# First three chunks projected from unpermuted weights by 32-column tiles, with the permutations behind them

## The chip, the cores and the metric

One core of one Trainium2 chip runs one program. The metric is the device time of that program in microseconds (us), and the figure of record is the median of several runs. TensorE (PE) multiplies matrices, its weight loads are shown as PEld; VectorE (DVE), ScalarE (ACT) and GpSimd (POOL) do the rest, and SyncE (SP) issues the transfers (DMAs).

## The reference

Four layers work on one sequence of 2048 tokens of width 576, in bfloat16: attention, gated linear unit (GLU), attention, GLU, each on a normalised input and added to it. The weights of the two attentions are the same, as are those of the two GLUs.

```python
def _A_ref(x, wqkv, wo):                 # 32 heads of 18, window of 8 at distance 2
    qkv = (x @ wqkv).reshape(B, S, 3, H, Dh)
    idx = pos[:, None] - (jnp.arange(8) * 2)[None, :]
    ...
    logits = jnp.einsum("bhsd,bhswd->bhsw", q, kg) * scale   # masked where idx < 0
    attn = softmax(logits)
    return einsum("bhsw,bhswd->bhsd", attn, vg).reshape(B, S, D) @ wo

def _B_ref(x, w_gate, w_up, w_down):     # F = 4608
    return ((x @ w_gate) * (x @ w_up)) @ w_down

x = x + _A_ref(_layernorm(x), wqkv, wo)
x = x + _B_ref(_layernorm(x), w_gate, w_up, w_down)
x = x + _A_ref(_layernorm(x), wqkv, wo)
x = x + _B_ref(_layernorm(x), w_gate, w_up, w_down)
```

## The kernel before

The sequence is cut into chunks of 128 tokens (the first four) or 256. For each chunk an attention and a GLU are made, and the chunks of the two layer pairs follow one another in one list, `seq`. All weights stay in SBUF: `wqkv` for the attention, `wg`, `wu` and `wgu_t` for the GLU (loaded in six slices of 768 columns, 0 to 5); the rows of w_down pass through seven buffers `wd`. Width 576 is four blocks of 128 rows and a tail of 64, so each contraction has four full matmuls (k = 0 to 3) and a half one.

The attention works with q, k and v in an order of columns in which the 18 elements of a head lie apart: column d * 32 + h in place of h * 18 + d. The kernel gets this order by permuting the weights once. `load_w` (L323) loads the raw `A_wqkv` into a scratch tile `scr` in two parts, "a" (q and k) and "b" (v), and `perm` in `setup_b` (L355) copies it, 512 columns of q, k or v at a time and the last 64 or 128 apart, with a read of every 18th element, into `wqkv`. DVE copies q and half of k, ACT the rest of k and all of v. `project` (L527) then multiplies: 14 column blocks of 128 per chunk, 56 full matmuls and 14 of 64 rows. For chunk 0 (`fast`) the q and k part runs k by k as the permuted blocks come, then the v part.

What follows for a chunk: eviction of q, k, v from PSUM (L609, L611, L638, L645); four products q*k for two window places each on DVE (L676), summed over d by PE with the selector `Esel` (L691, in tiles of 32 columns); softmax on DVE and ACT (L710 to L722); the weights spread over the heads' rows by PE with `Bsel` (L732) and copied back; eight products with v (L762), which for chunk 0 PE sums (L766, L767) and for others DVE; the output projection (L816), the residual (L786), statistics (L414, L418), normalisation (L439), transposes on PE (L452, L454) and their eviction (L457). Then the GLU: gate and up (L866, tails L877), `g_sb` (L901) and the product `h` (L902), down (L918, L919).

The order on every engine is not that of the source. Each step is an `op` with an engine, a cost in ns, what it reads and writes, a priority and a rank (the chunk's number; 0.5 for a permutation, 60 for GLU). `Plan.run` repeatedly takes the step that can start first by these costs, and holds a step of higher rank back if one of rank 0 or below would come within a guard time (`GUARD`). Where PE would stand idle, `fill` adds dummy matmuls (L1067). The result is written out in that order; at run time engines wait for one another by semaphores. All transfers of this stage go through SP's one queue, in order.

Chunks 0 to 4 have their input transposed on PE. Chunk 1's projection stands on PE just ahead of the first GLU matmul, those of chunks 2 and 3 follow behind the first six units of the GLU of chunk 0.

## Time and profile before

| what | value |
|---|---|
| three runs | 1060.21, 1063.39, 1062.1 us; median 1062.1 |
| profiled execution | 1063.46 us, span from first to last instruction 1061.7 us |
| granted PE clock, mean | 0.996 |
| PE, DVE, ACT busy | 98%, 74%, 39% of the span |
| DMA | 133.67 MB, mean 126 GB/s |

The profile is of one execution. Busy times are sums over instructions; matmuls overlap, and the end of one is modelled, so a stream of matmuls is read by its starts. A row of the timeline is start, duration, engine, line, operation, output and inputs, sizes, count, and in brackets the idle time ahead of it and what ended that. Lines are those of the kernel before; the changed kernel has other numbers (L527 becomes L610 for raw and L613 for permuted weights, L355 L417, L676 L762, L691 L777, L732 L818, L762 L850, L786 L874, L866 L954, L902 L990, L918 L1006).

### The profile page before, as it was taken

To read this page: it belongs to the slowest core of one execution; us is meant where nothing else is said; L and a number is where in the kernel's file an instruction comes from. 1 tells how busy PE (TensorE), PEld (TensorE's weight loads), DVE (VectorE), ACT (ScalarE), POOL (GpSimd) and SP (SyncE) were. 2 spreads that over 40 slices of the span, in tenths; PEclk is the share of its full clock that TensorE was granted. 3 is DMA by queue.
4 is the path that set the end of the run, shared out by engine and by line. 5 is a ranking of instruction groups with operands and counts; after the bars stand their busy time and mean duration, and the time that the engine had idled before them with its cause. 6 is when DMAs were issued, how large, how long until landed. Compare 5 with 4: busy or idle time off the path is not lost.

```text
span 1061.7 us, 39938 instructions
## 1 busy us (share of the span) xinstructions
PE 1044.4 (98%) x17864; PEld 839.5 (79%) x17864; DVE 781.6 (74%) x1421; ACT 411.8 (39%) x1090; POOL 8.9 (1%) x33
## 2 busy tenths in 40 slices
PE   7999999999999999999999999999999999999998
PEld 4888878798888878878878887777877778877775
DVE  7688979786969896989798874666788748833332
ACT  6752254342334534423444324324334252233231
POOL 3000000000000000000000000000000000000000
PEclk9999999999999999999999999999999999999999
DMA  9956563623253444345444443243362333443332
GB/s 263 323 184 197 179 178 102 170 69 121 81 147 86 128 103 109 82 126 138 117 93 106 110 143 94 83 147 87 75 173 82 94 94 115 126 127 102 114 102 68
DMA packets 146827, 133.67 MB, mean 126 GB/s; under 512 B 42272, under 2 KB 146016, under 8 KB 146656
## 3 DMA queue, kind: packets, MB, share of 16 engines
q1 hardware_dynamic: 146656, 131.13, 44.1%
q8 instruction: 139, 2.28, 0.9%
q14 instruction: 32, 0.26, 0.1%
HBM read 118.51 MB, written 4.06 MB: 115 GB/s over the span
## 4 chain that ended last, share of the span: by engine, by line
PE 77%; DVE 14%; DMA 5%; ACT 1%; SPq 1%; issue 1%; DVEq 0%; ACTq 0%
PE pu L890 15%; PE pg L890 13%; PE pu L958 5%; PE acct L890 4%; PE pa L958 4%; PE pa L890 4%; PE pg L527 4%; PE pu L527 3%; PE pg L958 3%; PE acct L958 3%; PE pu L866 3%; PE pg L866 3%; PE pg L918 3%; DVE scr L762 2%; DVE oT L776 2%; DVE h L902 2%
## 5 line engine op out<-in xcount | busy, mean ns | idle before, releaser
L890 PE MATMUL pg<-xnT_B,wg 64*128 64x256 bf16 x3072 | 394.8, 270 | 3.2 <-DVE xf L786 3.2
L890 PE MATMUL pu<-xnT_B,wu 64*128 64x256 bf16 x3072 | 394.3, 270 | 1.6 <-DVE xf L938 1.2
L890 PEld LDWEIGHTS <-wg 64*128 64x128 bf16 x4032 | 367.3, 94 | 28.6 <-issue 3.4
L890 PEld LDWEIGHTS <-wu 64*128 64x128 bf16 x4032 | 366.3, 94 | 24.6 <-issue 3.6
L902 DVE TENSOR_TENSOR h<-pu,g_sb 128x512 bf16<-128x512 f32 x228 | 153.7, 686 | 59.4 <-ACT g_sb L901 56.0
L958 PEld LDWEIGHTS <-h 64*128 64x128 bf16 (+1 forms) x1992 | 120.7, 94 | 96.9 <-DVE h L902 1.6
L901 ACT CAST g_sb<-pg 128x512 bf16<-128x512 f32 x228 | 132.2, 586 | 115.8 <-PE pg L890 80.6
L471 ACT COPY tok<-pu 1x1 f32<-1x1 f32 x270 | 39.7, 147 | 308.8 <-PE pu L890 214.5
L959 PE MATMUL pg<-wd,h 64*128 64x64 bf16 (+1 forms) x828 | 157.4, 190 | 1.4 <-DVE xf L786 1.4
L959 PE MATMUL pu<-wd,h 64*128 64x64 bf16 (+1 forms) x828 | 157.4, 190 | 0.3 <-DVE xf L786 0.2
L958 PE MATMUL pg<-wd,h 64*128 64x512 bf16 x600 | 154.9, 377 | 0.3 <-DVE h L902 0.3
L958 PE MATMUL pu<-wd,h 64*128 64x512 bf16 x600 | 154.9, 377 | 0.0
L890 PE MATMUL acct<-xnT_B,wg 64*128 64x256 bf16 x960 | 130.7, 269 | 0.0
L890 PE MATMUL pa<-xnT_B,wu 64*128 64x256 bf16 x960 | 130.7, 270 | 0.0
L959 PEld LDWEIGHTS <-h 64*128 64x128 bf16 (+1 forms) x1992 | 119.2, 95 | 2.1 <-issue 1.7
L527 PEld LDWEIGHTS <-wqkv 64*128 64x128 bf16 (+1 forms) x2044 | 103.9, 94 | 15.5 <-issue 3.8
L676 DVE TENSOR_TENSOR scr<-qT,kv 128x2560 bf16<-128x2560 bf16 (+1 forms) x68 | 89.9, 1326 | 29.9 <-ACT kv L611 29.7
L958 PE MATMUL acct<-wd,h 64*128 64x512 bf16 (+1 forms) x396 | 103.6, 382 | 0.4 <-DVE h L902 0.4
L958 PE MATMUL pa<-wd,h 64*128 64x512 bf16 (+1 forms) x396 | 104.0, 382 | 0.0
L890 PE MATMUL pu<-xnT_B,wgu_t 64*128 64x256 bf16 x384 | 103.5, 270 | 0.0
L890 PE MATMUL pg<-xnT_B,wgu_t 64*128 64x256 bf16 x384 | 103.5, 269 | 0.0
L527 PE MATMUL pg<-xnT_A,wqkv 64*128 64x256 bf16 (+2 forms) x853 | 96.3, 261 | 0.1
(155 smaller groups left out, 1645.9 us busy)
## 6 DMA issues: line engine op xcount, KB each, us to landing
wd<-in_B_w_down_dram SPq DMA_DIRECT2D x324, 288.0 KB, 4.5
scr<-a_dram SPq DMA_DIRECT2D x52, 128.0 KB, 2.8
wg<-in_B_w_gate_dram SPq DMA_DIRECT2D x6, 768.0 KB, 9.4
wu<-in_B_w_up_dram SPq DMA_DIRECT2D x6, 768.0 KB, 10.9
out_dram<-xf SPq DMA_DIRECT2D x16, 144.0 KB, 3.2
xb<-in_A_x_dram SPq DMA_DIRECT2D x6, 288.0 KB, 2.9
a_dram<-scr SPq DMA_DIRECT2D x13, 128.0 KB, 2.8
scr<-in_A_wqkv_dram SPq DMA_DIRECT2D x4, 288.0 KB, 4.3
```

Of the source, the lines that this page charges most:

```text
L471: box["at"] = nc.scalar.copy(tok[0:1, :], src())
L527: return nc.tensor.matmul(bank(p_, u)[0:m, e * n:(e + 1) * n], lhsT=wqkv[r_, k, w0:w0 + m], rhs=xnT_A[r_, k, c0:c0 + n], start=start, stop ...
L676: nc.vector.tensor_tensor(late["prod"][p_ % 2][:, :, :, 0:n], q2, k2, op=ALU.mult)
L762: nc.vector.tensor_tensor(js(dst), js(vT[:, :, o0:o0 + n]), abw, op=ALU.mult)
L776: op("DVE", 70 + 2.63 * n, lambda i_=i_: nc.vector.tensor_tensor(oT[:, :, 0:n], oT[:, :, 0:n], late["prod"][i_ % 2][:, 0, :, 0:n], op=ALU. ...
L866: nc.tensor.matmul(pt[:, e * n:(e + 1) * n], lhsT=w_[:, k, ft * P:(ft + 1) * P], rhs=xT[:, k, 0:n], start=(first and k == 0 and e == 0), s ...
L890: return nc.tensor.matmul(ps[:, e * n:(e + 1) * n], lhsT=w_, rhs=xT[rows, k, 0:n], start=(first and e == 0 and k == 0), stop=(not first an ...
L901: op("ACT", 490, lambda: nc.scalar.copy(g_sb[gs][:, 0:ul], pg[use["slot"]][:, 0:ul]), r=[f"wg_{j}_{u}"], w=[f"g{gs}"], prio=0, due=True)
L902: op("DVE", 605, lambda: nc.vector.tensor_tensor(hb[hs][:, 0:ul], pu[use["slot"]][:, 0:ul], g_sb[gs][:, 0:ul], op=ALU.mult), r=[f"wu_{j}_{ ...
L918: nc.tensor.matmul((pg, pu)[i][use["slot"]][:], lhsT=lhs, rhs=wt[:, e % 2, 0:512], start=first, stop=fin)
L958: return [lambda: nc.tensor.matmul((pg, pu)[i][use["slot"]][:], lhsT=lhs, rhs=wt[rows, e % 2, 0:512], start=first, stop=fin, skip_group_ch ...
L959: lambda: nc.tensor.matmul((pg, pu)[i][tl["slot"]][:, 0:TL], lhsT=lhs, rhs=wt[rows, e % 2, 512:D], start=first, stop=fin, skip_group_check ...
```

## The change

1. The raw weights are no longer in `scr` but in the place of the GLU weights' slices 4 and 5 (`raw`). Those slices' loads come later, after every use of the raw weights; `setup_glu` is split for this.
2. Chunks 0, 1 and 2 (`NRAW = 3`) project straight from the raw weights: each block of 128 columns is made by four matmuls of 32 columns into four 32-row parts of the bank, each with weights read at every 18th column (`raw32`).
3. The permutations get rank 1 and priority 6 and go, step by step, to DVE or ACT, whichever is free first (`alts`). Only chunk 3 and later read `wqkv`.
4. The planner first plans the operations of rank below 1 alone (`ahead`) and keeps the start of each as `res`; in the real pass an operation of a later rank may not be placed where it would run over such a place by more than `TOL`. Guards get shorter. Attentions of chunks 1 and 2 are put into the list ahead of GLU 0.
5. Small steps of chunk 0: statistics in single operations, normalisation and eviction of the GLU's input in two halves on ACT and DVE, four product buffers instead of two in the sum over v, x of chunk 1 loaded ahead of the weights, part "b" issued after the second instead of the third piece of "a".

```diff
-HOLD = 2
+HOLD = 1
-GUARD = {"DVE": 300, "ACT": 300, "PE": 600, "POOL": 0, "SP": 0}
+GUARD = {"DVE": 50, "ACT": 50, "PE": 100, "POOL": 0, "SP": 0}
+TOL = {"DVE": 100, "ACT": 100, "PE": 100, "POOL": 1e9, "SP": 1e9}
...
+    def ahead(self, slots, last):
+        every, emit = self.ops, self.fill
+        ops = [o for o in every if o.idx < last and o.rank < 1]
...
+        self.run(slots)
...
+        for o in ops:
+            if o.rank == 0 and o.cost and o.eng != "SP":
+                o.res = o.end - o.cost
...
+                if o.rank >= 1 and o.cost:
+                    for b0, c0, _, _ in book[o.eng]:
+                        if t + o.cost > b0 + shift + TOL[o.eng] and t < b0 + shift + c0:
+                            t = b0 + shift + c0
...
-    wrawa = scr[:, 0:KT * 2 * D].rearrange("p (k n) -> p k n", k=KT)
-    wrawb = scr[:, 7168:7168 + KT * D].rearrange("p (k n) -> p k n", k=KT)
+    R0 = 4 * F // FS
+    def raw(t3, k):
+        if k == KF:
+            return wu[:, t3, R0 + D:R0 + 2 * D]
+        return wg[:, k, R0 + t3 * D:R0 + (t3 + 1) * D] if t3 < 2 else wu[:, k, R0:R0 + D]
+    def raw32(r_, k, c):
+        t3, d = (c // 512, c % 512 // 32) if c < 1536 else ((c - 1536) // 64, 16 + (c - 1536) % 64 // 32)
+        return raw(t3, k)[r_].rearrange("p (h d) -> p d h", h=H)[:, d]
...
-            perm("DVE", 530, f"wq0_{k}", 0, ra)
-            perm("DVE", 180, f"wq3_{k}", 3, ra)
...
+                    parts, costs = [(dst, src)], {"DVE": 560, "ACT": 1020}
...
+                box["o"] = op("ACT", costs["ACT"], fn, r=rk, w=[key], prio=6, alts=costs)
...
-    def setup_glu():
+    def setup_glu(ss):
...
-                   w=[f"{nm}{s}"], nbytes=P * KF * fw * 2, prio=4 + s)
+                   w=[f"{nm}{s}"] + rawk * (s >= 4), nbytes=P * KF * fw * 2, prio=4 + s)
...
+            if halves:
+                op("ACT", 490, lambda i=i: nc.scalar.activation(xn[ia + i][:, 0:320], src(i)[:, 0:320], ACT.Identity,
...
+                op("DVE", 330, lambda i=i: nc.vector.tensor_scalar(xn[ia + i][:, 320:D], src(i)[:, 320:D], rstd[:, ia + i:ia + i + 1],
...
-            wk = [f"wq{t}_{k}" for t in tw for k in range(KT)]
+            wk = rawk if j < NRAW else [f"wq{t}_{k}" for t in tw for k in range(KT)]
...
+                if j < NRAW:
+                    for jj in range(4):
+                        nc.tensor.matmul(bank(p_, u)[32 * jj:32 * jj + 32, e * n:(e + 1) * n], lhsT=raw32(r_, k, w0 + 32 * jj), rhs=xnT_A[r_, k, c0:c0 + n],
+                                         start=start, stop=stop, skip_group_check=True)
+                    return
...
+            pb = (i_ // 2) % 2 if fast else 0
+            pk = [f"prod{i_ % 2}{pb}"] if fast else [f"prod{i_ % 2}0", f"prod{i_ % 2}1"]
...
     load_x(0, 1)
     setup_a()
+    load_x(1, 1)
     load_w("a")
-    load_x(1, 1)
     load_w("b")
...
-    setup_glu()
+    setup_glu(range(4))
...
-        attention(j, l, t0, nst)
+        if j >= NRAW or j == 0:
+            attention(j, l, t0, nst)
+        if j == 0:
+            boot = len(pl.ops)
+            for j2 in range(1, NRAW):
+                pool["k"], pl.rank = "pa", j2
+                attention(j2, *seq[j2])
+            setup_glu(range(4, FS))
...
-        pl.run({**{k: len(v) for k, v in banks.items()}, "unit": NB - 1})
+        room = {**{k: len(v) for k, v in banks.items()}, "unit": NB - 1}
+        pl.ahead(room, boot)
+        pl.run(room)
```

More of the change, by code (lines that the diff above doesn't have):

```diff
@@ L18 @@
     __slots__ = ("eng", "cost", "fn", "deps", "order", "succ", "n", "prio", "idx", "hold", "free",
-                 "lat", "margin", "ready", "end", "nbytes", "use", "pair", "need", "rank", "late", "half")
+                 "lat", "margin", "ready", "end", "nbytes", "use", "pair", "need", "rank", "late", "half", "land", "res", "alts")
 POOLQ = False
-HOLD = 2
-VP = ["ACT"] * 5
-VT = ["ACT"] * 5
+HOLD = 1
 SLACK = {"DVE": 500, "ACT": 300, "PE": 0, "POOL": 0, "SP": 0}
 IDLE = (2000, 300)
-GUARD = {"DVE": 300, "ACT": 300, "PE": 600, "POOL": 0, "SP": 0}
+GUARD = {"DVE": 50, "ACT": 50, "PE": 100, "POOL": 0, "SP": 0}
 TURN = (148, 98)
+TOL = {"DVE": 100, "ACT": 100, "PE": 100, "POOL": 1e9, "SP": 1e9}
 LOOK = {"DVE": 1, "ACT": 1, "PE": 1, "POOL": 0, "SP": -9}
@@ L47, in op @@
     def op(self, eng, cost, fn, r=(), w=(), prio=1, after=None, hold=None, free=None, margin=0, nbytes=0, use=None,
-           pair=None, need=None, due=False, late=0, half=False):
+           pair=None, need=None, due=False, late=0, half=False, land=False, alts=None):
         o = Op()
+        o.land, o.res, o.alts = land, None, alts
         o.rank, o.late, o.half = -1 if due else self.rank, late, half
@@ L82, in also @@
                     o.n += 1
+    def ahead(self, slots, last):
+        every, emit = self.ops, self.fill
+        ops = [o for o in every if o.idx < last and o.rank < 1]
+        uses = {id(u): u for o in ops for u in (o.use, o.need, *(o.pair or ())) if u is not None}
+        was = [(u, dict(u)) for u in uses.values()]
+        ns = [(o, o.n) for o in every]
+        fns = [(o, o.fn) for o in ops]
+        for o in ops:
+            o.fn = lambda: None
+        self.ops, self.fill = ops, None
+        self.run(slots)
+        self.ops, self.fill = every, emit
+        for o, f in fns:
+            o.fn = f
+        for u, v in was:
+            u.clear()
+            u.update(v)
+        for o, n in ns:
+            o.n = n
+        for o in ops:
+            if o.rank == 0 and o.cost and o.eng != "SP":
+                o.res = o.end - o.cost
     def run(self, slots):
+        live = set(self.ops)
+        book = {e: sorted((o.res, o.cost, o.idx, o) for o in self.ops if o.res is not None and o.eng == e) for e in self.LAT}
+        shift = 0.0
         clock = {e: 0.0 for e in self.LAT}
@@ L93, in run @@
             urgent = {}
+            gate = [(o.idx, max([p.ready for p in o.deps], default=0.0)) for o in cand if o.land]
             for o in cand:
+                if o.alts:
+                    o.eng = min(o.alts, key=lambda e: (clock[e] + o.alts[e], e))
+                    o.cost, o.lat = o.alts[o.eng], self.LAT[o.eng]
                 t = 0.0
                 for p in o.deps:
-                    e = p.ready if p.eng != o.eng else p.end
+                    e = p.ready if p.eng != o.eng or o.land else p.end
                     if e > t:
@@ L100, in run @@
                 t += o.margin
+                for i, g in gate:
+                    if o.eng == "SP" and o.idx > i:
+                        t = max(t, g + 100)
                 if o.hold is not None:
@@ L118, in run @@
             o = best[1]
-            if o.rank > 0:
+            if o.rank > 0 and o.cost >= 100:
                 end = best[0][0] + o.cost
@@ L159, in run @@
                     free[o.free].append((u["last"], u["slot"]))
+            if o.res is not None:
+                book[o.eng].remove((o.res, o.cost, o.idx, o))
+                shift = max(0.0, t - o.res)
             o.fn()
@@ L163, in run @@
                 s.n -= 1
-                if s.n == 0:
+                if s.n == 0 and s in live:
                     cand.append(s)
@@ L204 @@
     NXS, NWD, NH, NXB, NB = 4, 7, 6, 3, 3
+    NRAW = 3
     consts = ctx.enter_context(tc.tile_pool(name="consts", bufs=1))
@@ L305, in load_x @@
         op("SP", 470, dma(dst[:, i0:i0 + nst, :], xv[:, t0:t0 + nst, :]), w=[f"{key}{i}" for i in range(i0, i0 + nst)],
-           nbytes=P * nst * D * 2, prio=0 if t0 < 1 else 1.5 if t0 < 2 else 2.5)
+           late=300 if 1 < t0 < 4 else 0, nbytes=P * nst * D * 2, prio=0 if t0 < 2 else 2.5)
     def setup_a():
@@ L318, in load_w @@
     def load_w(c):
-        wr, c0, c1 = ((wrawa, 0, 2 * D), (wrawb, 2 * D, 3 * D))[c == "b"]
+        c0, c1 = ((0, 2 * D), (2 * D, 3 * D))[c == "b"]
         for k in range(KT):
@@ L322, in fn @@
                 def fn(k=k, r_=r_, rows=rows):
-                    i = nc.sync.dma_start(wr[r_:r_ + rows, k, :], A_wqkv[k * P:k * P + rows, c0:c1])
+                    src = A_wqkv[k * P:k * P + rows, c0:c1]
+                    if c == "b":
+                        dst = raw(2, k)[r_:r_ + rows]
+                    elif k < KF:
+                        dst = wg[:, k, R0:R0 + 2 * D]
+                    else:
+                        dst, src = wu[r_:r_ + rows, 0:2, R0 + D:R0 + 2 * D], src.rearrange("p (t n) -> p t n", t=2)
+                    i = nc.sync.dma_start(dst, src)
                     if c == "a" and k == HOLD:
@@ L327, in fn @@
                         tc.add_manual_dep(i.ins, held["w"].ins.name, sync)
-                op("SP", 470, fn, r=[f"wrawa{HOLD}"] if c == "b" and k == 0 else [], w=[f"wraw{c}{k}"] if k < KF else [f"wrawt{c}{r_}"],
-                   nbytes=rows * (c1 - c0) * 2, prio=1 + (c == "b"), late=700 if c == "a" else 0)
+                wait = c == "b" and k == 0
+                held["o"] = op("SP", 470, fn, r=[f"wrawa{HOLD}"] * wait, land=wait, w=[f"wraw{c}{k}"] if k < KF else [f"wrawt{c}{r_}"],
+                   nbytes=rows * (c1 - c0) * 2, prio=1 + (c == "b"), late=(420, 1000, 900, 1200, 1250)[k] if c == "a" else 300)
     def setup_b():
@@ L342, in setup_b, with perm @@
         op("POOL", 2600, mk_zero, w=[f"{x}{t}{i}" for x in "qkv" for t in (4, "H") for i in ZN] + [f"halo{i}" for i in range(n_al)] + ["wo_z"])
+        pl.rank = 1
         for k in range(KT):
-            def perm(eng, cost, key, t3, rk, k=k):
+            def perm(key, t3, rk, k=k):
                 if t3 < 3:
-                    wr = wrawb[:, k, :] if t3 == 2 else wrawa[:, k, t3 * D:(t3 + 1) * D]
-                    src = wr.rearrange("p (h d) -> p d h", h=H)[:, 0:16, :]
+                    src = raw(t3, k).rearrange("p (h d) -> p d h", h=H)[:, 0:16, :]
@@ L348, in perm @@
                     dst = wqkv[:, k, t3 * 512:(t3 + 1) * 512].rearrange("p (d h) -> p d h", h=H)
+                    parts, costs = [(dst, src)], {"DVE": 560, "ACT": 1020}
                 else:
-                    t0, t1 = (0, 2) if t3 == 3 else (2, 3)
-                    src = (wrawa, wrawb)[t3 - 3][:, k, :].rearrange("p (t h d) -> p t d h", t=t1 - t0, h=H)[:, :, 16:18, :]
-                    dst = wqkv[:, k, 3 * 512:3 * D].rearrange("p (t d h) -> p t d h", t=3, h=H)[:, t0:t1]
-                fn = {"DVE": nc.vector.tensor_copy, "POOL": nc.gpsimd.tensor_copy, "ACT": nc.scalar.copy}[eng]
@@ L354, in perm @@
-                pl.rank = 0.5
-                op(eng, cost, lambda: fn(dst, src), r=rk, w=[key], prio=2 + (t3 in (2, 4)))
-                pl.rank = 0
-            ra, rb = [[f"wraw{c}{k}"] if k < KF else [f"wrawt{c}0", f"wrawt{c}{TL}"] for c in "ab"]
-            perm("DVE", 530, f"wq0_{k}", 0, ra)
-            perm("DVE", 180, f"wq3_{k}", 3, ra)
-            if k % 2:
-                perm("DVE", 530, f"wq1_{k}", 1, ra)
-            else:
-                perm("ACT", 1000, f"wq1_{k}", 1, ra)
@@ L364, in setup_b @@
-            perm(VP[k], {"ACT": 1050, "DVE": 560, "POOL": 1250}[VP[k]], f"wq2_{k}", 2, rb)
-            perm(VT[k], {"ACT": 330, "DVE": 200, "POOL": 300}[VT[k]], f"wq4_{k}", 4, rb)
+                    tt = (0, 1) if t3 == 3 else (2,)
+                    parts = [(wqkv[:, k, 1536 + 64 * t:1600 + 64 * t].rearrange("p (d h) -> p d h", h=H),
+                              raw(t, k).rearrange("p (h d) -> p d h", h=H)[:, 16:18, :]) for t in tt]
+                    costs = {"DVE": 110 * len(tt), "ACT": 200 * len(tt)}
@@ new lines, in perm, with fn @@
+                box = {}
+                def fn():
+                    for d_, s_ in parts:
+                        {"DVE": nc.vector.tensor_copy, "ACT": nc.scalar.copy}[box["o"].eng](d_, s_)
+                box["o"] = op("ACT", costs["ACT"], fn, r=rk, w=[key], prio=6, alts=costs)
+            ra, rb = [[f"wraw{c}{k}"] if k < KF else [f"wrawt{c}0", f"wrawt{c}{TL}"] for c in "ab"]
+            perm(f"wq0_{k}", 0, ra)
+            perm(f"wq1_{k}", 1, ra)
+            perm(f"wq3_{k}", 3, ra)
+            perm(f"wq2_{k}", 2, rb)
@@ L367, in mk_sel @@
+            perm(f"wq4_{k}", 4, rb)
+        pl.rank = 0
         def mk_sel():
@@ L382, in setup_b @@
         op("POOL", 1000, mk_cap, w=["cap"], prio=3.5)
-        op("DVE", 0, lambda: None, r=[f"wq{t}_{k}" for t in (0, 1, 3) for k in range(KT)], w=["prod0", "prod1", "s10", "Lt"])
-        op("ACT", 0, lambda: None, r=[f"wq{t}_{k}" for t in (2, 4) for k in range(KT)], w=["s11", "s12", "ab"])
     def setup_wo():
@@ L392, in setup_wo @@
             op("SP", 470, dma(wo_p[32 * dd:32 * dd + 32, KF, :], wv_[:, 16 + dd, :]), w=[f"wot{dd}"], nbytes=32 * D * 2, prio=2.6)
-    def setup_glu():
+    rawk = [f"wraw{c}{k}" for c in "ab" for k in range(KF)] + [f"wrawt{c}{r_}" for c in "ab" for r_ in (0, TL)]
+    def setup_glu(ss):
         fw = F // FS
-        for s in range(FS):
+        for s in ss:
             fs = slice(s * fw, (s + 1) * fw)
@@ L422, in head @@
                 continue
+            if on_pe:
+                for a in range(2):
+                    op("DVE", 400, lambda a=a, i=i: nc.vector.bn_stats(out=st[:, ia + i, a, :], in_=src(i)[:, a * HD:(a + 1) * HD]),
+                       r=[keys[i]], w=[f"st{ab}{ia + i}{a}"], prio=prio)
+                op("DVE", 210, lambda i=i: nc.vector.bn_aggr(out=mv[:, ia + i, :], in_=st[:, ia + i]),
+                   r=[f"st{ab}{ia + i}0", f"st{ab}{ia + i}1"], w=[f"mv{ab}{ia + i}"], prio=prio)
+                continue
             op("DVE", 970, stats, r=[keys[i]], w=[f"mv{ab}{ia + i}", f"st{ab}{ia + i}0", f"st{ab}{ia + i}1"], prio=prio)
@@ L433, in head @@
         op("DVE", 75, lambda: nc.vector.scalar_tensor_tensor(nmr[:, sl], mv[:, sl, 0], -1.0, rstd[:, sl], op0=ALU.mult, op1=ALU.mult),
-           r=mk + rk, w=nk, prio=prio)
+           r=mk + rk, w=nk, prio=0 if on_pe else prio)
         for i in range(nst):
@@ L441, in apply @@
                     nc.scalar.activation(y[:, D:D + TL], x[:, KF * P:D], ACT.Identity, **sc)
-            op("ACT", 770 if on_pe else 1100, apply, r=[keys[i], nk[i], rk[i]], w=[f"xn{ab}{ia + i}"], prio=prio)
+            if halves:
+                op("ACT", 490, lambda i=i: nc.scalar.activation(xn[ia + i][:, 0:320], src(i)[:, 0:320], ACT.Identity,
+                                                                bias=nmr[:, ia + i:ia + i + 1], scale=rstd[:, ia + i:ia + i + 1]),
+                   r=[keys[i], nk[i], rk[i]], w=[f"xn{ab}{ia + i}"], prio=prio)
+                op("DVE", 330, lambda i=i: nc.vector.tensor_scalar(xn[ia + i][:, 320:D], src(i)[:, 320:D], rstd[:, ia + i:ia + i + 1],
+                                                                   nmr[:, ia + i:ia + i + 1], op0=ALU.mult, op1=ALU.add),
+                   r=[keys[i], nk[i], rk[i]], w=[f"xn{ab}{ia + i}h"], prio=prio)
+            else:
+                op("ACT", 770 if on_pe else 1100, apply, r=[keys[i], nk[i], rk[i]], w=[f"xn{ab}{ia + i}"], prio=prio)
             cs = slice(c0 + i * P, c0 + (i + 1) * P)
@@ L454, in tr @@
                     nc.tensor.transpose(bf(b())[r_:r_ + TL, KF, :], xn[ia + i][:, KF * P:D], ident[:])
-            o = op("PE", 290, tr, r=[f"xn{ab}{ia + i}", "ident"], prio=0, margin=mg, **b.take())
+            o = op("PE", 290, tr, r=[f"xn{ab}{ia + i}", "ident"] + [f"xn{ab}{ia + i}h"] * halves, prio=0, margin=mg, **b.take())
             pl.also(o, [key + str(ia + i)])
+            if halves:
+                b.use["left"] = 2
+                op("ACT", 420, lambda i=i, b=b, cs=cs: nc.scalar.copy(dst[:, 0:3, cs], bf(b())[:, 0:3]), r=[b.key], w=[key + str(ia + i)],
+                   prio=prio, **b.drop())
+                op("DVE", 330, lambda i=i, b=b, cs=cs: nc.vector.tensor_copy(dst[:, 3:KT, cs], bf(b())[:, 3:KT]), r=[b.key], w=[key + str(ia + i) + "h"],
+                   prio=prio, **b.drop())
+                continue
             op("ACT", 590, lambda i=i, b=b, cs=cs: nc.scalar.copy(dst[:, :, cs], bf(b())), r=[b.key], w=[key + str(ia + i)],
@@ L567, in project @@
                 for part in (0, 1):
-                    u, parts, ts = (ua, au + bu[4:5], (0, 1, 3)) if part == 0 else (ub, bu[:4] + bu[5:], (2, 4))
+                    u, parts = (ua, au + bu[4:5]) if part == 0 else (ub, bu[:4] + bu[5:])
                     key = (ka, kb)[part]
@@ L583, in project @@
                         o = op("PE", 57 * len(parts) if k < KF else 190 + 28 * len(parts), fn,
-                               r=xk + [f"wq{t}_{k}" for t in ts], w=[key], prio=0, **kw)
+                               r=xk + ([f"wraw{'ab'[part]}{k}"] if k < KF else [f"wrawt{'ab'[part]}{r_}" for r_ in (0, TL)]), w=[key], prio=0.5 * part, **kw)
                         if k == 0 and part == 0:
@@ L598, in pieces @@
                     return o
-                o1 = pieces(ua, au, ka, True, False, late["wo"] if 2 <= j < 4 else None, margin=400, pair=(ua, ub))
-                o2 = op("PE", 190 + 0.215 * n * len(tl), lambda: tails(True), r=xk + wk, w=[ka, kb], prio=0, after=o1, need=ub)
+                o1 = pieces(ua, au, ka, True, False, late["wo"] if 2 <= j < 4 else None, margin=400, pair=(ua,) if j == 1 else (ua, ub))
+                o2 = op("PE", 190 + 0.215 * n * len(tl), lambda: tails(True), r=xk + wk, w=[ka, kb], prio=0, after=o1, **(dict(pair=(ub,)) if j == 1 else dict(need=ub)))
                 pieces(ub, bu, kb, False, True, o2)
@@ L693, in esel @@
                                          stop=(i_ == len(srcs()) - 1), skip_group_check=True)
-            pk, sk = f"prod{p_ % 2}", f"s1{p_}"
-            op("DVE", 70 + 5.2 * n, l1, r=qk, w=[pk], prio=prio)
+            pk, sk = [f"prod{p_ % 2}0", f"prod{p_ % 2}1"], f"s1{p_}"
+            op("DVE", 70 + 5.2 * n, l1, r=qk, w=pk, prio=prio)
             if fast:
@@ L698, in attention @@
                 op("PE", 20 * 20, lambda p_=p_: esel(p_, lambda: [late["prod"][p_ % 2][:, :, k, :] for k in range(KT)]),
-                   r=["sel", pk], prio=0, **kw)
+                   r=["sel", *pk], prio=0, **kw)
             else:
-                op("DVE", 82 + 2.02 * n, l2, r=[pk], w=[pk], prio=prio)
-                op("DVE", 276 + 2.02 * n, l3, r=[pk], w=[sk], prio=prio)
+                op("DVE", 82 + 2.02 * n, l2, r=pk, w=pk, prio=prio)
+                op("DVE", 276 + 2.02 * n, l3, r=pk, w=[sk], prio=prio)
         if not fast:
@@ L757, in attention, with pv @@
             to_o = i_ == 0 and not fast
-            def pv(i_=i_, o0=o0, to_o=to_o):
+            pb = (i_ // 2) % 2 if fast else 0
+            pk = [f"prod{i_ % 2}{pb}"] if fast else [f"prod{i_ % 2}0", f"prod{i_ % 2}1"]
+            def pv(i_=i_, o0=o0, to_o=to_o, pb=pb):
                 abw = late["ab"][:, :, 0:W * sq].rearrange("p j (w s) -> p j w s", w=W)[:, :, i_].unsqueeze(1).to_broadcast([P, KT, 4, sq])
-                dst = oT[:, :, 0:n] if to_o else late["prod"][i_ % 2][:, 0, :, 0:n]
+                dst = oT[:, :, 0:n] if to_o else late["prod"][i_ % 2][:, pb, :, 0:n]
@@ L762, in pv, with gather @@
                 nc.vector.tensor_tensor(js(dst), js(vT[:, :, o0:o0 + n]), abw, op=ALU.mult)
-            def gather(i_=i_):
-                pr = late["prod"][i_ % 2][:, 0]
+            def gather(i_=i_, pb=pb):
+                pr = late["prod"][i_ % 2][:, pb]
                 nc.tensor.matmul(bo[0]()[:, 0:KF * n], lhsT=ident[:], rhs=pr[:, 0:KF, 0:n], start=(i_ == 0), stop=(i_ == W - 1))
                 nc.tensor.matmul(bo[1]()[:, 0:n], lhsT=ident[:], rhs=pr[:, KF, 0:n], start=(i_ == 0), stop=(i_ == W - 1))
-            op("DVE", 70 + 2.63 * n, pv, r=vk + abk, w=["oT"] if to_o else [f"prod{i_ % 2}"], prio=prio)
+            op("DVE", 70 + 2.63 * n, pv, r=vk + abk, w=["oT"] if to_o else pk, prio=prio)
@@ L769, in attention @@
             if fast:
                 if i_ == 0:
-                    ob0 = op("PE", 0, lambda: None, w=[bo[1].key], prio=0, hold=bo[1].pool, use=bo[1].use)
-                    op("PE", 330, gather, r=["prod0", "ident"], w=[bo[0].key, bo[1].key], prio=0, hold=bo[0].pool, use=bo[0].use)
+                    ob0 = op("PE", 0, lambda: None, r=abk, w=[bo[1].key], prio=0, hold=bo[1].pool, use=bo[1].use)
+                    op("PE", 330, gather, r=[*pk, "ident"], w=[bo[0].key, bo[1].key], prio=0, hold=bo[0].pool, use=bo[0].use)
@@ L773, in attention @@
                 else:
-                    op("PE", 330, gather, r=[f"prod{i_ % 2}", "ident"], w=[bo[0].key, bo[1].key], prio=0)
+                    op("PE", 330, gather, r=[*pk, "ident"], w=[bo[0].key, bo[1].key], prio=0)
             elif i_:
                 op("DVE", 70 + 2.63 * n, lambda i_=i_: nc.vector.tensor_tensor(oT[:, :, 0:n], oT[:, :, 0:n], late["prod"][i_ % 2][:, 0, :, 0:n],
-                                                                        op=ALU.add), r=[f"prod{i_ % 2}"], w=["oT"], prio=prio)
+                                                                        op=ALU.add), r=pk, w=["oT"], prio=prio)
@@ L849, in glu @@
         fk = [f"xf{(t0 // 2) % NXS}_{i0 + i}" for i in range(nst)]
-        xT, xk = xnT_B[j % NXB], [f"xB{j % NXB}_{i}" for i in range(nst)]
+        xT, xk = xnT_B[j % NXB], [f"xB{j % NXB}_{i}" for i in range(nst)] + ["xB0_0h"] * (j == 0)
         ul = fpu * n
```

## The prediction

> **What bounds the kernel now.** First the page's busy row, then the table of windows over the first 50 us. Columns after the window: its length, each engine's busy us with its instructions, the granted clock, the DMA share, GB/s.

> ```profile
> PE 1044.4 (98%) x17864; PEld 839.5 (79%) x17864; DVE 781.6 (74%) x1421; ACT 411.8 (39%) x1090; POOL 8.9 (1%) x33
> 0.00:10.00 10.00, 7.29 (x54) 3.76 (x54) 6.54 (x17) 6.32 (x9) 8.92 (x33) 1.00 0.81 229
> 10.00:20.00 10.00, 8.42 (x132) 4.69 (x130) 8.87 (x22) 8.03 (x17) 0.00 (x0) 0.83 1.00 254
> 20.00:30.00 10.00, 8.66 (x72) 5.29 (x71) 8.39 (x24) 5.93 (x14) 0.00 (x0) 1.00 1.08 311
> 30.00:40.00 10.00, 9.73 (x173) 8.46 (x171) 5.95 (x16) 7.37 (x18) 0.00 (x0) 1.00 1.08 338
> 40.00:50.00 10.00, 10.00 (x184) 8.82 (x182) 6.10 (x15) 7.37 (x17) 0.00 (x0) 1.00 1.07 330
> ```

> PE is full from about 30 us on. So only two things pay: an earlier first matmul of chunk 0's GLU (after it PE hardly waits), and less PE work behind it. Before it PE runs few useful matmuls (132 and 72 a window against 184); part of its busy time there is the dummies of L1067. What sets that start is the chain of chunk 0, read in the timeline:

> ```profile
> 10.27 0.35 PEld L527 LDWEIGHTS <-wqkv 64*128 64x128 bf16 x9 [0.25 <-DVE wqkv L355]
> 12.38 3.03 DVE L676 TENSOR_TENSOR scr<-qT,kv 128x1280 bf16<-128x1280 bf16 x4
> 15.32 0.81 DVE L414 BATCH_NORM_STATS2 st<-xb 128x6 f32<-128x288 bf16 x2
> 19.17 0.42 DVE L722 TENSOR_TENSOR scr<-scr,zs 128x256 bf16<-128x256 f32 x1
> 19.50 0.22 PEld L527 LDWEIGHTS <-wqkv 64*128 64x128 bf16 x5 [0.56 <-ACT wqkv L355]
> 20.90 0.38 PE L732 MATMUL pu<-scr,Bsel 128*128 128x256 bf16 x2 [0.24 <-ACT scr L611]
> 22.15 3.94 DVE L762 TENSOR_TENSOR scr<-kv,scr 128x640 bf16<-128x640 bf16 x8
> 28.02 0.46 DVE L786 TENSOR_TENSOR xf<-pg,xb 128x288 f32<-128x288 f32 x1
> 33.88 1.07 PE L866 MATMUL pg<-xnT_B,wg 128*128 128x128 bf16 x16
> ```

> The brackets name what ended a wait: twice a permutation copy (L355, on DVE for q and k, on ACT for v), once the eviction of the first attention bank. The GLU starts at 33.88.

> **The change, part by part.**

> *Start of the logits.* The tails of q and k now wait for their load alone. Before, the last such load was issued at 3.71 and took at most 5.4 us to land, 9.1; it now stands behind one more x load (0.46 us of the queue): about 9.6, tails done at 10.05 instead of 10.74. But DVE's second k cast now follows ACT's eviction of the same bank (its wait stands in the new order), 0.3 us. So 0 to -0.7; I take -0.4.

> *Softmax.* Stats (0.81) and aggregate (0.21) of another tile stood between the logits and the first softmax step. Now they are single operations: one of 0.4 stays there, the others go behind, one into the wait for ACT's exponential. -0.6.

> *Spread and v.* From the end of L722 (19.59) to the first product (22.15) were 2.56 us: the second spread matmul waited for the first's bank, and v's evictions, late after ACT's 4 us of permutations, shared ACT. Now v is projected by about 13 and the two spreads follow one another into two banks: 0.16 to PE, 0.4 matmul, two evictions of 0.6 and 0.7 half overlapped, 1.55 in all. -1.0.

> *Products.* Eight of 0.49 took 3.94, since each pair waited for PE to empty one of two buffers (four waits of 0.18 on PE tell of it). With four buffers they run back to back at 0.41: 3.36. -0.6.

> *Residual to GLU.* 28.02 to 33.88 is 5.86. The one-element multiply no longer stands behind stats (-0.3), the normalisation of 0.87 is shared by ACT and DVE (-0.3), PE's transposes of another chunk (0.5) no longer stand ahead of the first GLU matmul. The two halves of the eviction run one after the other (a wait of ACT on DVE): +0.1. Two operations of chunk 1's logits are placed ahead of the residual but fit while it waits for PE. -0.85 (bounds 0 and -1.1).

> Together -3.45: the GLU at about 30.4.

> *Work that leaves the full stretch.* In the new order chunk 2's projection stands ahead of the GLU; before, two projections of 70 matmuls followed it. One runs from 40.64 to 44.5: -3.8.

> *What is added on PE.* 168 groups of four 32-column tiles with 128 rows replace 168 full matmuls, and 21 double groups of 64 rows the tails: 189 periods. No row shows a 32-column load with columns 36 bytes apart, so its price needs bounds. Nearest are PE's own small tiles with contiguous weights, beside full matmuls:

> ```profile
> 185.31 0.41 PE L691 MATMUL pg<-scr,Esel 128*32 128x128 bf16 x16
> 38.86 1.06 PE L866 MATMUL pg<-xnT_B,wg 128*128 128x128 bf16 x16
> ```

> Sixteen small ones in 0.41, less one completion of 0.22, leave 0.19 over three steps of a group: about 60 ns. Sixteen full ones: (1.06 - 0.22)/15 = 56 ns. So four tiles with their four loads run side by side and cost what one full matmul does. For the stride, the copies of the same data:

> ```profile
> L355 ACT COPY wqkv<-scr 128x512 bf16<-128x512 bf16 x8 | 8.8, 1114 | 0.7 <-DMA scr<-in_A_wqkv_dram 0.7
> L355 DVE COPY wqkv<-scr 128x512 bf16<-128x512 bf16 x7 | 4.7, 691 | 0.0
> ```

> 1114/512 = 2.2 ns an element on ACT, 691/512 = 1.35 on DVE, so 43 to 70 ns for 32 columns. Side by side that hides under 56, or makes the period 70 at most (189 x 14 ns = +2.7 us). One after another it is 4 x 43 to 4 x 70, 173 to 279 ns: +22 to +42 us. I take side by side and 57 ns, +0.2, because the row of PE's own loads is nearest.

> [...]

> *Clock.* The page's window 10 to 20 has 0.83: 3.4 us at half rate, late in that stretch, when only dummies suffered. Chunk 1's projection, 70 periods from 15.2 on (3.6 us at full clock), now lies there, and the spread follows it on PE just when L722 is ready (18.6). PE is no busier ahead of it than before, so I expect the drop again: 0 to +1.9, taken as +1.5.

> *Behind the scenes.* The permutations still begin early on idle engines, but nothing of the first three chunks waits for them; on ACT four of 1.1 us fall after the spread. The last must end before chunk 3's projection, at about 38.8; by the order it follows three GLU evictions (34 to 37) and should end near 38.1. If it slips, PE waits as long. GLU slices 4 and 5 overwrite the raw weights, so their first load on SP waits for chunk 2's projection and for permutations; behind it stand down weights. In the old run the queue was full to 60 us (share 1.07, then 0.23 for 60 to 70) and PE needed those down weights at 70.5: some 10 us of cover, of which the 7 gained use most. The planner's second pass (planned places) emits nothing; it only orders.

> Sum: -3.45 - 3.8 + 0.2 + 1.5 = -5.55, say -5.6. The profiled execution took 1063.46 (span 1061.7), 1.4 above the median of 1062.1; I apply the difference to the median: **1056.5**.

> **The rivals.**

> *Slower loads, side by side no longer enough (same).* Every ns over 56 costs 0.19 us, nearly all on the path, since both raw projections end just when PE is next needed. With the clock loss the gain shrinks under 3.2 us (0.3%, what a measurement of this kernel can tell) at a period near 69 and is gone at 86: 1059 to 1065. For: ACT's 70 ns. Against: DVE's 43.

> *Loads one after another (slower).* If the strided reads of the four tiles share one way into the array, the period is 4 x 43 = 173 or more: 1056.5 + 0.19 x 116 = 1078, up to 1099. It decides from 86 ns on (94 without clock loss). For: no strided load is in the trace. Against: the Esel row.

> [...]

> *No clock drop (faster still).* 1055; and if the front gains a little more, 1053.5, below which the down weights stop it.

> *The earlier start does not come (little gain).* If ACT's or the loads' waits take the place of the permutations', only the 3.8 us remain, less the clock: about 1060.

> **How the numbers follow.** Forecast with period 56 to 65, clock lost or not: 0.62, all faster (1053.5 to 1058.5). Period 65 to 100: 0.16, split 0.08 faster, 0.04 same, 0.04 slower. No earlier start: 0.08, same. Loads one after another: 0.14, slower. So faster 0.70, same 0.12, slower 0.18. Low is 1053.5; high 1064 takes in periods to about 95.

> **What would show it.** Right: the L954 line's first GLU matmul near 30 to 32; 16 raw matmuls (L610) in about 0.4; products near 3.4; one projection of 70 behind the GLU's start. Wrong: raw groups above 70 ns, spread (L818) well past 20.5, PE waiting for the last permutation at 38 or for down weights at 60 to 65.

## The result, and the profile after

The changed kernel takes 1075.2 us (median of four runs, 1073.2 to 1078.4) against 1062.55 for the kernel before in the same comparison: ratio 1.0125, interval 1.0095 to 1.0156. It is slower by 1.25%, where 0.5% faster was forecast. The profiled execution took 1073.17 us, with a span of 1071.4 against 1061.7.

The busy row and the table of windows, here from 10 us on, answer to those shown of before; the columns are the same.

```profile
PE 1044.6 (98%) x18474; PEld 836.2 (78%) x18474; DVE 782.5 (73%) x1423; ACT 413.4 (39%) x1095; POOL 9.0 (1%) x33
10.00:20.00 10.00, 6.39 (x287) 5.31 (x287) 6.60 (x14) 6.41 (x17) 0.00 (x0) 0.92 0.86 222
20.00:30.00 10.00, 3.43 (x176) 3.00 (x168) 2.11 (x6) 2.44 (x4) 0.00 (x0) 0.84 1.04 315
30.00:40.00 10.00, 9.63 (x181) 6.34 (x184) 7.87 (x20) 7.18 (x15) 0.00 (x0) 0.73 1.08 328
40.00:50.00 10.00, 6.41 (x230) 5.46 (x223) 4.61 (x15) 3.54 (x9) 0.00 (x0) 0.83 0.85 249
```

The busy sum of PE has not changed (1044.6 against 1044.4), yet from 20 to 30 us PE works 3.43 of 10 us, and DVE and ACT work less than 2.5: nobody is busy and nobody waits for a transfer of data. The granted clock is under 1 in four windows running, 0.68 of a window short in all. In windows of 1 us it is 0.50 from 19 to 21, 29 to 35 and 46 to 49 us, so the 0.68 are 13.6 us at half rate. PE's timeline over the same stretch shows what it stands at. The x column counts matmuls, and each has one weight load beside it.

```profile
18.13 0.46 PE L777 MATMUL pu<-scr,Esel 128*32 128x64 bf16 x32 [1.45 <-issue]
18.36 1.94 PE L610 MATMUL pg<-xnT_A,wg 128*32 128x128 bf16 x64
20.05 1.10 PE L610 MATMUL pu<-xnT_A,wg 128*32 128x128 bf16 x32
23.23 0.73 PE L610 MATMUL pu<-xnT_A,wg 128*32 128x128 bf16 x32 [2.07 <-issue]
...
29.97 0.87 PE L610 MATMUL pg<-xnT_A,wu 128*32 128x128 bf16 x24 [4.50 <-issue]
30.77 0.61 PE L818 MATMUL pg<-scr,Bsel 128*128 128x256 bf16 x2
...
38.55 1.27 PE L610 MATMUL pg<-xnT_A,wg 128*32 128x128 bf16 x64
39.63 1.24 PE L610 MATMUL pu<-xnT_A,wg 128*32 128x128 bf16 x64
...
48.89 1.14 PE L954 MATMUL pg<-xnT_B,wg 128*128 128x128 bf16 x16
```

PE stops in the middle of a projection, waiting for "issue", that is for nothing that the profile names. Between the two stops at 18.13 and 23.23 lie 32 + 64 + 32 = 128 matmuls, with their loads 256 instructions. From 23.23 to 29.97 there are again 256, and the next stop ends 512 further on, at 44.96. The spread (L818) stands behind the second and third stop on PE and runs at 30.77 where it ran at 19.83; the GLU (L954) starts at 48.9 in place of 33.9. PE's table of waits from 8 to 50 us gives the sum:

```profile
PE pg L610 <- issue: 9.4, 3, 4.5
PE pu L610 <- issue: 2.1, 1, 2.1
PE pu L777 <- issue: 1.4, 1, 1.4
```

12.9 us in five stops. The section of the page on DMA queues tells what comes in 256s.

```profile
q8 instruction: 144, 2.36, 0.9%
```

Before, q8 moved 139 packets and 2.28 MB. PE then ran 17864 matmuls and as many loads, 35728 instructions: 257 to a packet, 64 bytes each. Now it runs 36948, and 36948 x 64 is 2.36 MB. From these counts I take q8 to carry PE's own instructions, 256 to a block; no row says so. The trace has every packet of q8 at 16384 bytes, and the time of each, to be set beside the stops (us):

| PE goes on at | its block's packet starts | packet lasts | end of packet to PE | since PE last went on |
|---|---|---|---|---|
| 12.48 | 9.52 | 1.54 | 1.42 | |
| 18.13 | 15.62 | 0.98 | 1.53 | 5.65 |
| 23.23 | 20.59 | 0.92 | 1.71 | 5.10 |
| 29.97 | 27.43 | 1.18 | 1.36 | 6.74 |
| 44.96 | 42.39 | 1.10 | 1.47 | |

Every stop ends 1.4 to 1.7 us after the end of such a packet, and the next packet follows 2.5 to 4.2 us after PE has entered a block (1.65 us after the last stop). From 8 to 50 us q8 has seven packets and PE enters seven blocks; each packet starts 1.0 to 4.2 us after PE has entered a block, one to a block. What asks for it no row shows. The places of the stops fit blocks of 256 instructions: counted in matmuls from the start of the kernel, they stand before numbers 224, 352, 480, 608 and 863, 128 apart or twice that (863 is one short; a few records can be missing from a trace). The kernels below that stop for issue for longer than 0.7 us up to 70 us do so at these numbers or one short of them, and at 735 and 991, at whatever time they reach them. 128 full matmuls of 56 ns last 7.2 us, longer than this way takes; 32 groups of four small tiles last about 2.

### The profile page after: what moved, and what is told of

Same layout as the page of the kernel before. It is cut to its first block, busy times and chain, and to the rows that moved or that the text cites. A ratio compares the mean times of both kernels' runs of the same rounds, so it can differ in the third digit from the quotient of the medians.

```text
span 1071.4 us, 41151 instructions
## 1 busy us (share of the span) xinstructions
PE 1044.6 (98%) x18474; PEld 836.2 (78%) x18474; DVE 782.5 (73%) x1423; ACT 413.4 (39%) x1095; POOL 9.0 (1%) x33
## 3 DMA queue, kind: packets, MB, share of 16 engines
q8 instruction: 144, 2.36, 0.9%
## 4 chain that ended last, share of the span: by engine, by line
PE 84%; DVE 10%; DMA 3%; issue 2%; ACT 1%; SPq 0%; POOL 0%; DVEq 0%; POOLq 0%; ACTq 0%
PE pu L978 16%; PE pg L978 15%; PE pu L1046 5%; PE acct L978 5%; PE pa L978 5%; PE pa L1046 5%; PE pg L1046 5%; PE pg L613 3%; PE pu L954 3%; PE acct L1046 3%; PE pg L954 3%; PE pu L613 3%; PE pg L1006 3%; DVE oT L864 2%; DVE scr L850 2%
## 5 line engine op out<-in xcount | busy, mean ns | idle before, releaser
L1046 PEld LDWEIGHTS <-h 64*128 64x128 bf16 (+1 forms) x1992 | 118.8, 94 | 99.3 <-DVE h L990 2.1
L1047 PEld LDWEIGHTS <-h 64*128 64x128 bf16 (+1 forms) x1992 | 117.0, 95 | 2.4 <-issue 2.0
L762 DVE TENSOR_TENSOR scr<-qT,kv 128x2560 bf16<-128x2560 bf16 (+1 forms) x68 | 89.9, 1325 | 26.1 <-ACT kv L697 25.9
L613 PEld LDWEIGHTS <-wqkv 64*128 64x128 bf16 (+1 forms) x1834 | 91.9, 94 | 11.3 <-issue 1.5
L864 DVE TENSOR_TENSOR oT<-oT,scr 128x1280 bf16<-128x1280 bf16 (+1 forms) x119 | 90.9, 764 | 3.3
```

What stands on the lines that cost most here:

```text
L613: return nc.tensor.matmul(bank(p_, u)[0:m, e * n:(e + 1) * n], lhsT=wqkv[r_, k, w0:w0 + m], rhs=xnT_A[r_, k, c0:c0 + n], start=start, stop ...
L762: nc.vector.tensor_tensor(late["prod"][p_ % 2][:, :, :, 0:n], q2, k2, op=ALU.mult)
L864: op("DVE", 70 + 2.63 * n, lambda i_=i_: nc.vector.tensor_tensor(oT[:, :, 0:n], oT[:, :, 0:n], late["prod"][i_ % 2][:, 0, :, 0:n], op=ALU. ...
L1046: return [lambda: nc.tensor.matmul((pg, pu)[i][use["slot"]][:], lhsT=lhs, rhs=wt[rows, e % 2, 0:512], start=first, stop=fin, skip_group_ch ...
L1047: lambda: nc.tensor.matmul((pg, pu)[i][tl["slot"]][:, 0:TL], lhsT=lhs, rhs=wt[rows, e % 2, 512:D], start=first, stop=fin, skip_group_check ...
```

## The experiments

The theory: four times the instructions per projection, and blocks of 256 that do not come fast enough. The rivals: the strided reads of the weights, and the new order of the work with its planned places. The first four runs separate them: the number of instructions and the distance of the columns are changed one without the other. The edits are shown shortened.

**One full matmul on adjacent columns**

```diff
-for jj in range(4):
-    nc.tensor.matmul(bank(p_, u)[32 * jj:32 * jj + 32, ...], lhsT=raw32(r_, k, w0 + 32 * jj), ...)
+nc.tensor.matmul(bank(p_, u)[0:128, ...], lhsT=raw(t3, k)[r_, x:x + 128], ...)
```

> Each group of four 32-column tiles becomes one full matmul on 128 adjacent raw columns; the order of the columns within a head is left out in chunks 0 to 2. A projection is 70 load-matmul pairs again in place of 280. Instruction supply (the stalls of 1.3 to 4.5 us in the raw projections end where a block of 256 PE instructions arrives): no stall over 1 us among them, first GLU matmul at 30 to 32 us in place of 48.9, time 1055 to 1058. Strided reads as the cost: the same, 1055 to 1058. Order of the work as the cost: the GLU still starts late, 1070 or more.

Measured: ratio to the kernel before 0.9957 (0.9942 to 0.9972), 1055.9 us. All the order of the change is in it, and the 13 us of stops are gone:

```profile
15.30 1.07 PE L611 MATMUL pg<-xnT_A,wg 128*128 128x128 bf16 x16
...
18.68 0.38 PE L819 MATMUL pg<-scr,Bsel 128*128 128x256 bf16 x2
...
30.44 1.05 PE L955 MATMUL pg<-xnT_B,wg 128*128 128x128 bf16 x16
```

The order is not the cause: with full matmuls in the same places the spread comes at 18.7 and the GLU at 30.4.

**One full matmul on columns 18 bytes apart**

```diff
+src = wg[r_, k, R0 + 2 * t3 + x // 128:R0 + 2 * t3 + x // 128 + 127 * 9 + 1:9]   # k < KF
```

> One full matmul per block again, but its 128 weight columns lie 18 bytes apart (every 9th column of the raw q and k part, for k = 0 to 3; tails adjacent; the right order of columns is left out in chunks 0 to 2). Instruction supply: as with adjacent columns, GLU from 30 to 32 us, 1055 to 1058. Strided reads as the cost: periods well over 56 ns, 100 or more, and 168 of them: GLU 5 us or more later, 1062 or more.

Measured: 0.9965 (0.9952 to 0.9979), 1056.8 us, GLU at 31.9. Sixteen matmuls take (28.23 - 27.27) / 16 = 60 ns each in place of 56. The distance costs little here.

**Four tiles on adjacent columns**

```diff
-lhsT=raw32(r_, k, c)
+lhsT=raw(t3, k)[r_, x:x + 32]
```

> Four 32-column tiles for each block as in the change, so the same number of instructions, but on adjacent columns (the order of the columns within a head is left out in chunks 0 to 2). Instruction supply: nothing is gained, four or five stalls of 1 to 5 us exactly 256 PE instructions apart, GLU at 45 to 49 us, 1072 to 1077. Strided reads as the cost: 1056 to 1059, no stalls.

Measured: 1.0133 (1.0102 to 1.0164), 1075.2 us, as slow as the change. GLU at 45.8, stops of 1.75 and 4.55 us in chunk 1's projection and 4.72 in chunk 2's, and 3.06 behind the first GLU matmuls. It is the number of instructions, not the distance. The distance has a price of its own, though: 16 groups of four last (17.30 - 16.40) us here, 56 ns a group, and (39.63 - 38.55) us in the changed kernel, 67.5 ns. That is 11.5 ns for each of 189 periods, 2.2 us.

**The count alone, in the kernel before**

```diff
+if j in (2, 3):
+    for jj in range(4):
+        nc.tensor.matmul(bank(p_, u)[32 * jj:32 * jj + 32, ...], lhsT=wqkv[r_, k, w0 + 32 * jj:w0 + 32 * jj + 32], ...)
+    return
```

> The kernel before, with one edit: the projections of chunks 2 and 3, which lie in PE's full stretch, are made by four 32-column tiles for each block on the permuted, adjacent weights; the output is complete. Instruction supply: 420 more load-matmul pairs are over three more blocks of 256 instructions, each ending in a stall of 3 to 5 us between 41 and 66 us, first GLU matmul unmoved at 33.9, 1074 to 1082. If tiles cost only their run time beside one another, or if it was the change's order that lost the time, 1061 to 1064.

Measured: 1.0151 (1.0136 to 1.0166), 1075.9 us; the GLU starts at 33.9 as before. The loss lies where the tiles are:

```profile
49.12 0.29 PE L529 MATMUL pu<-xnT_A,wqkv 64*32 64x128 bf16 x2 [5.43 <-issue]
...
56.14 1.31 PE L529 MATMUL pg<-xnT_A,wqkv 128*32 128x128 bf16 x58 [3.51 <-issue]
...
59.87 0.29 PE L529 MATMUL pu<-xnT_A,wqkv 64*32 64x128 bf16 x2 [0.48 <-issue]
...
63.33 0.46 PE L529 MATMUL pu<-xnT_A,wqkv 128*32 128x128 bf16 x18 [1.50 <-issue]
```

Each of these goes on a block after the one before it: 7.0, 3.7 and 3.5 us apart. The windows between them show what differs (the last three columns are the granted clock, the DMA share and GB/s):

```profile
49.12:56.14 7.02, 3.51 (x128) 3.05 (x128) 2.22 (x5) 2.81 (x7) 0.00 (x0) 0.70 0.95 284
56.14:59.87 3.73, 3.25 (x128) 2.86 (x128) 0.00 (x0) 0.00 (x0) 0.00 (x0) 0.58 0.05 16
59.87:63.33 3.46, 1.96 (x130) 1.70 (x130) 0.00 (x0) 1.07 (x2) 0.00 (x0) 0.96 0.02 5
```

With the DMA queues full (a share of 0.95) a block takes 7 us, with them all but idle (0.02) 3.5, and even that is longer than the 2 us in which PE runs it. Neither the new order nor the raw weights are in this kernel.

**The same, with the DMA queues quiet**

```diff
-    setup_glu(range(4)) ... load_wd()           # ahead of attention 0
+    setup_glu((4, 5, 0, 1, 2, 3)) ... load_wd() # behind attentions 1 and 2, slices 4 and 5 first
```

> The changed kernel, but the loads of the GLU weights' six slices and of the first w_down buffers are put behind the last use of the raw weights on SP's queue, slices 4 and 5 first, so that the DMA engines are nearly idle while the raw projections run. The GLU must start later and the time be worse, 1075 to 1095; what counts is the stalls at each 256th PE instruction. If the blocks of instructions wait behind bulk transfers, the time from one resumption to the next falls from 5.1 to 6.7 us to under 4 us and the stalls of 3.6 and 4.5 us to under 2; the raw projection of chunk 1 ends before 22 us in place of 26 to 31. If a block takes as long by itself, stalls and spacing stay as they are.

One run, 1079.9 us. The windows from one stop to the next, and the stops:

```profile
17.79:22.07 4.28, 3.07 (x129) 2.96 (x128) 3.29 (x9) 2.82 (x5) 0.00 (x0) 0.67 0.43 120
22.07:26.34 4.27, 2.26 (x128) 2.04 (x128) 0.06 (x1) 1.07 (x2) 0.00 (x0) 1.00 0.41 122
```

```profile
22.07 0.74 PE L610 MATMUL pu<-xnT_A,wg 128*32 128x128 bf16 x32 [1.21 <-issue]
...
26.34 0.62 PE L610 MATMUL pg<-xnT_A,wu 128*32 128x128 bf16 x24 [2.01 <-issue]
```

PE goes on at 17.79, 22.07 and 26.34: every 4.3 us, not under 4 as expected, and not 5.1 to 6.7 either. The DMA queues were quieter, not idle: a share of 0.43 and 0.41 in these stretches. From entering a block to the next packet's start are now 1.1 to 1.9 us instead of 2.5 to 4.2; the packet takes no less than before (0.9 to 1.8 us), and the 1.4 us behind it stay. The stops between 8 and 50 us fall from 12.9 us to 5.7 (3.6 + 1.2 + 0.9). So the wait was longer beside bulk transfers, in these two kernels and in the kernel before with tiles, but no block that PE stopped for came sooner than 3.5 us after the one ahead of it, in any run here: by these numbers a free queue would have made the stops shorter and not ended them.

**Less of it**

```diff
-    NRAW = 3
+    NRAW = 1    # and, in a second kernel, 2
```

> NRAW = 1: only chunk 0 is projected from raw weights, by 32-column tiles; the output is complete. Instruction supply: one block boundary in the projection and one in the logits, 1.3 and 1.5 us, no stall ahead of the spread; GLU at 36 to 39 because chunk 1's projection now waits for permutations of low rank, 1061 to 1064. Raw tiles slow by themselves: about a third of the loss of the change, 1065 or more.

> NRAW = 2: chunks 0 and 1 from raw weights by 32-column tiles; the output is complete. Instruction supply: the stalls of chunk 1's projection (2.1 and 4.5 us) are there and push the spread to about 30, those of chunk 2's are not: GLU at 40 to 44, 1066 to 1071.

Measured: with one chunk 1.0007 (0.9998 to 1.0017), 1062.2 us, GLU at 38.7, one stop of 0.8 us among PE's waits for issue; with two 1.0105 (1.0090 to 1.0120), 1071.6 us, just above the 1071 expected, GLU at 43.5, stops of 8.7 us. Most of the loss comes with the second chunk; its tiles follow the first chunk's and the selector matmuls closely. In that profile the granted clock was 0.75, 0.50 and 0.73 in the windows from 10 to 40 us, too, and what of the loss is clock and what is stops was not taken apart. (With one chunk the GLU starts 4.8 us later than before and the time is the same, since two projections besides chunk 0's, in place of one, then stand ahead of it.)

**Half the tiles**

```diff
+for jj in range(2): ... wg[r_, k, R0 + d:R0 + d + 63 * 18 + 1:18]   # 64 columns 36 bytes apart
+for jj in range(2): ... raw(t3, k)[r_, x:x + 64]                    # second kernel: adjacent
```

> Two tiles of 64 columns for each block in place of four of 32, read at a stride of 36 bytes in the q and k part for k = 0 to 3 (16 bytes elsewhere); the right order of columns is left out in chunks 0 to 2. 140 load-matmul pairs a projection. Instruction supply by blocks of 256: a projection is a little over one block, fetched in about 5 to 6 us and run in 4, so one stall of 1 to 2 us, GLU from 33 to 36, 1058 to 1061. A cost that grows with every extra pair: a third of the 19 us that separate four tiles from one, 1062 or 1063. Strided reads as the cost: 1065 or more.

> Two tiles of 64 adjacent columns for each block (order of columns left out in chunks 0 to 2). The two tiles of 64 strided columns took 124 to 126 ns a block without a stall. If the distance of 36 bytes made that, the pair now takes about 56 ns and the GLU starts near 31; if two tiles of 64 columns do not run side by side, 115 ns or more and the GLU at 39 to 42.

Measured: strided 1.0024 (1.0010 to 1.0037), 1063.5 us, no stop, but 124 ns for a pair of tiles and the GLU at 42.0. The 1058 to 1061 expected of instruction supply missed, and the time alone decides nothing: it lies between the 1062 or 1063 of a cost for each extra pair and the 1065 of strided reads. The 124 ns without a stop, and the second kernel, point to the distance. Adjacent columns (one run): 1055.2 us beside 1060.7 for before, 57 ns a pair, GLU at 32.0:

```profile
27.43 1.08 PE L611 MATMUL pg<-xnT_A,wg 128*64 128x128 bf16 x32
28.35 1.06 PE L611 MATMUL pu<-xnT_A,wg 128*64 128x128 bf16 x32
```

Twice the instructions cost next to nothing: a wait of 0.7 us for issue is left behind the GLU's start. Four times cost 13 us of stops. Why 36 bytes double the pair of 64 and add only a fifth to four tiles of 32 was not found out.

**What is left without the raw projection**

```diff
-    NRAW = 3
+    NRAW = 0    # permutations at rank 0.5, on the engines that had them
```

> All of the change but its raw projection: NRAW = 0, so every chunk multiplies the permuted weights, the permutations come at rank 0.5 on the engines that had them before; planned places, four product buffers, halves and the places of the raw weights stay. The output is complete. Instruction supply: no stalls, GLU at about 31, 1059 to 1061 (chunk 2's projection stays in the full stretch). Order of the work as the cost: slower than before, 1065 or more.

> All of the change but the raw projection again, with more rounds, to settle whether it beats the kernel before: the first runs gave a ratio of 0.9983. GLU at 31.6 in place of 33.9: 1.5 to 3 us faster, ratio 0.997 to 0.999.

Measured: 0.9983 (0.9967 to 0.9999) and again 0.9990 (0.9981 to 0.9999), 1058.9 and 1059.5 us: 1.2 us faster than the kernel before in both comparisons, the best complete version here. GLU at 31.6 and 32.2.

**Four product buffers alone, in the kernel before**

```diff
-late["prod"][i_ % 2][:, 0, :, 0:n]
+late["prod"][i_ % 2][:, (i_ // 2) % 2 if fast else 0, :, 0:n]
```

> The kernel before with one edit: the sum over v of chunk 0 goes through four product buffers in place of two; the output is complete. By the prediction's term the eight products shrink by 0.6 us and the GLU starts 0.6 to 0.9 earlier: ratio 0.9990 to 0.9995. If DVE's products were not what the residual waits for: no change.

Measured: 1.0007 (0.9998 to 1.0016). The eight products last 3.30 us in place of 3.94 and the GLU starts 0.4 earlier (33.46), but no gain in time can be measured. Where the 0.4 us go was not settled.

## Why the prediction was wrong, point by point

**The step that failed** is in "What is added on PE": "So four tiles with their four loads run side by side and cost what one full matmul does", and with it "+0.2". The tiles do run side by side: 56 ns a group on adjacent columns. But the step priced a group by how long PE runs it and took for granted that PE has the instructions. 840 load-matmul pairs in place of 210 are 630 pairs more, and 128 pairs are a block that took 5.1 to 6.7 us to come and about 2 to run. The 12.9 us of stops are this term, which no rival named. The row it rested on, sixteen Esel tiles, was too short to show it: 32 instructions of a block of 256.

**The stride** was inside its bounds: 67.5 ns between 56 and 70, +2.2 us where +0.2 was taken. Reads 18 bytes apart cost 60 against 56, 36 bytes apart 67.5 against 56, or 124 against 57 in tiles of 64.

**The rival "loads one after another"** gave 1078, close to the time, by a mechanism that did not happen: its groups would take 173 ns, and they took 67.5 in the changed kernel and 56 on adjacent columns. That the number came near is luck.

**The earlier start** was right, as the kernel of full matmuls on adjacent columns shows. Logits: first L691 at 13.26 before, 12.71 there, -0.55 (forecast -0.4). Spread: 19.83 to 18.68, -1.15 with the softmax in it (-0.4 and -0.6, together -1.0). Products: 3.94 to 3.4 (3.4); the waits of 0.18 on PE, by which the prediction argued this, are three and not four. First residual to GLU: 5.86 to 5.02, -0.84 (-0.85). GLU: 33.88 to 30.44, -3.44 (-3.45). Each is within 0.2 us of its forecast, so this sum is no luck.

**Chunk 2's projection** does stand ahead of the GLU there (210 projection matmuls ahead of it, 140 before). Its whole time, 0.9957 of before or -4.6 us (-6.2 to -3.0), holds the forecast of -5.55, but that is partly luck: the sum had +1.5 for a clock drop that this trace does not have (1.00 in each window to 50 us), and without it gives -7.05, which the interval does not reach. Where the rest of the gain went was not looked into.

**The clock** in the changed kernel is another matter than foretold. Not 3.4 us but 13.6 us run at half rate: the 64 tiles that start at 18.36 take 1.94 us at 0.50 and those at 38.55 take 1.27 at 1.00, the same work. The three stretches up to 50 us begin at 18.4, 28.6 and 45.7 us, two just after PE goes on (18.13, 44.96) and one inside the stop of 4.50; the kernel before has one of 3.4 us there, at 15.8, with no stop for issue. What brings them was not shown. GLU at 48.89 less 30.44 is 18.45 us; 12.9 are stops and 2.2 the stride, and the 3.4 that are left fit the slow clock, which was not taken apart from other waits.

**Behind the scenes**: among PE's waits after 28 us none is for a permutation (L417), as forecast. Whether the down weights would have stopped an early GLU cannot be seen here; with the GLU at 30.4 PE did not wait for them up to 90 us.

**The range** ended at 1064, at a period of 95 ns, and the time lies 11 us above it.

## What to carry to other kernels

Count instructions, not only their run time: a change that cuts a matmul into small tiles multiplies what PE must be sent, and in these runs 256 instructions took 3.5 us to come at best and 7 when the DMA queues were full. The instruction queue's row in the profile of the kernel before shows the size of a block (2.28 MB in 139 packets, 16 KB each; over 35728 instructions, 64 bytes each). Work out how long PE takes to run one block in the densest stretch: where a stretch of several blocks used each up in about 2 us, sooner than the 3.5 to 7 in which they came, PE stopped. A stretch of little more than one block, as in the kernel with half the tiles, got by. Wait rows that name only "issue", 256 or 512 instructions from each other, were its mark here.
